# Norm factors of q and k: from GpSimd's power to ScalarE's logarithm and exponential with a Newton step on VectorE, and new due times for the planner

## The chip, the cores and the metric

The kernel runs on one core of one Trainium2 chip. Its time is the device time in microseconds (us) of one execution; of several executions the median is given. A profiled execution adds a trace: every instruction of TensorE (PE; PEld is its weight load), VectorE (DVE), ScalarE (ACT) and GpSimd (POOL), and the DMA issues of SyncE (SP), with start and duration.

## The reference

Attention with normalised q and k, for 8 batches of 12 heads, 448 positions and 64 columns a head, then a two-layer network with `h * cos(h)` between its matmuls:

```python
def rmsnorm(x, g):
    rms = np.sqrt(np.mean(x * x, axis=-1, keepdims=True) + 1e-06)
    return x / rms * g
q_n, k_n = (rmsnorm(q, g_q), rmsnorm(k, g_k))
scores = scale * np.matmul(q_n, k_n.transpose(0, 1, 3, 2))
scores = scores - np.max(scores, axis=-1, keepdims=True)
attn = np.exp(scores)
attn = attn / (np.sum(attn, axis=-1, keepdims=True) + 1e-09)
return np.matmul(attn, v)
...
h = x @ w_in          # 3584 x 768 by 768 x 2048
g = h * np.cos(h)
return g @ w_out
```

All tensors are 32-bit floats. What this case is about is `1 / rms`, one factor for each row of q and of k.

## The kernel before

**Units of work.** Two heads make a pair; there are 48 pairs, 6 for each batch. Pairs 0 to 5 are "plain" (32-bit matmuls without a split), pairs 6 to 47 split each operand into a high and a low part. For each pair the kernel prepares q and k (`prepare`), then attends (`attend`: scores, row minimum, exponential, transposes, product with v). `multiply` is the first matmul of the network for a batch; its result goes to memory. A second part, behind the attention pool, does `h * cos(h)` and the second matmul; the diff does not touch it.

**The factors.** For pairs 2 to 47, `st_square` (ACT) squares a tile `sd` of 128 x 14 x 64, `st_reduce` (DVE) sums it over 64 into `r` (128 x 14: seven columns for q, seven for k), and `st_pow` (POOL, L396 to L400) adds the small constant and raises to the power -0.5. Pairs 0 and 1 have 7 columns in `r`, and for k a path of their own: `kn_square`, `kn_reduce`, `kn_pow` (L426 to L429) on `rn` (112 x 8), then `kn_norm` (DVE, multiplies the rows of k), `kn_turn` (PE, transposes them) and `kn_copy` (ACT), and only then the scores. From pair 2 on, the k half of `r` goes to memory (`st_store`), comes back spread over the partitions (`rk_spread` into `D`, or `rk_load`), and `k_norm` (POOL) multiplies k by it into the tile `km` or in place. The q half of `r` is used in `rowmin` (DVE, L572), which multiplies the scores by it and takes the row minimum; `expo` (ACT, L580) follows.

**The order.** Each step is an entry with an engine, a cost, a due time, and the buffers that it reads and writes (`add`). `Plan.order` keeps a queue for each engine: of the entries that are ready when the engine is free, the one with the earliest due time goes next. What comes out is a fixed order of instructions for each engine; on the chip each engine takes them strictly in that order. Due times come from `base(u)` (13 apart for the plain pairs, 19 for the others) plus a table, `SHIFT`, with three numbers for each step (late pairs, the first split pairs, the plain pairs or the first network block), plus `PAIR` for single pairs; `BEGIN` moves the earliest start of loads. The weights of the network arrive as 64-bit numbers and are decoded in four steps on ACT, POOL, DVE and DVE (`decode`, L264, L267, L269, L271), among the early attention.

```python
def st_pow(u):
    n = st_cols(u)
    r = pair[u]["r"][:, :n]
    nc.gpsimd.tensor_scalar(r, r, 1.0, D * 1e-6, op0=ALU.mult, op1=ALU.add)
    nc.gpsimd.tensor_tensor(r, r, nhalf.broadcast_to([128, n]), ALU.pow)
```

Of the kernel before, what the change touches and what calls it, by code (L numbers as in the profile page):

```python
# [170 lines left out]
def tile_attention_moe(  # L171
# [11 lines left out]
    nc = tc.nc  # L183
# [212 lines left out]
    def st_pow(u):  # L396
        n = st_cols(u)
        r = pair[u]["r"][:, :n]
        nc.gpsimd.tensor_scalar(r, r, 1.0, D * 1e-6, op0=ALU.mult, op1=ALU.add)
        nc.gpsimd.tensor_tensor(r, r, nhalf.broadcast_to([128, n]), ALU.pow)  # L400
# [25 lines left out]
    def kn_pow(u):  # L426
        r = pair[u]["rn"][:KB]
        nc.gpsimd.tensor_scalar(r, r, 1.0, D * 1e-6, op0=ALU.mult, op1=ALU.add)
        nc.gpsimd.tensor_tensor(r, r, nhalf[:KB].broadcast_to([KB, 8]), ALU.pow)  # L429
# [406 lines left out]
    def y_store(b, oc, src):  # L836
# [10 lines left out]
        "k_norm": (47.04, -6.7, 6.09), "kn_copy": (0.0, 0.0, -26.03), "kn_load": (0.0, 0.0, -2.19),
        "kn_norm": (0.0, 0.0, 3.59), "kn_pow": (0.0, 0.0, -0.07), "kn_reduce": (0.0, 0.0, -6.89),
        "kn_square": (0.0, 0.0, 8.12), "kn_turn": (0.0, 0.0, -1.84), "kq_load": (-19.1, -5.97, 0.0),
        "m_place": (16.85, -8.49, 0.0), "pt_copy0": (0.0, 0.0, 23.54), "pt_copy1": (0.0, 0.0, 24.72),  # L850
        "pt_high0": (-18.32, 9.46, 0.0), "pt_high1": (-67.92, -9.7, 0.0), "pt_low0": (-20.7, 22.61, 0.0),
        "pt_low1": (-7.13, -11.08, 0.0), "q_high": (-127.36, -6.2, 0.0), "q_load": (0.0, 0.0, 72.1),
        "q_low": (-2.05, -0.3, 0.0), "q_scale": (-31.45, -11.91, 0.0), "rk_load": (8.49, 36.82, 0.0),
        "rk_spread": (0.0, 0.0, 11.66), "rowmin": (32.13, 70.56, 15.65), "rs_copy": (17.64, 0.91, 3.82),
        "rs_load": (-3.79, 6.46, 0.16), "rs_store": (8.77, 0.0, 5.61), "rsum": (-17.77, -6.78, 29.09),
        "score": (-0.07, -13.79, 0.0), "score_plain": (0.0, 0.0, -12.75), "st_load": (9.08, -3.06, -1.37),
# [5 lines left out]
        "w_decode": (208.02, 0.0, 0.0), "w_load": (3.35, 0.0, 0.0), "w_low": (13.11, 0.0, 0.0),
        "x_half": (4.91, 0.31, 0.0), "x_norm": (3.99, -11.02, 0.0), "x_plain": (0.0, 0.0, -20.3),
        "x_split": (-12.03, 9.82, 0.0), "x_sum": (7.41, -3.55, 0.0),
    }
    PAIR = (-10.16, 0.63, -1.81, -2.95, 0.29, 13.98, -17.36, -34.9, -15.47, 2.79, -35.19, -0.07)
    BEGIN = {"v_load": -14.52, "v_fetch": -9.53, "st_load": -5.75, "w_load": 12.81, "v_plain": 7.79, "kq_load": -31.08, "q_load": 2.47, "k_load": 4.72}

    def add(eng, cost, due, fn, *args, **more):
# [484 lines left out]
```

## Time and profile before

| what | value |
|---|---|
| median of 3 executions | 1363.93 us (1362.8 to 1364.56) |
| profiled execution, its own time | 1364.09 us |
| its span, first to last instruction | 1362.3 us |
| PE, DVE, ACT, POOL busy, share of the span | 98%, 75%, 68%, 47% |
| mean granted clock of TensorE | 0.997 of full speed |

Busy time counts an engine as busy while any of its instructions runs. The row of clock digits on the page shows 9 (full) throughout; a finer view of single stretches shows where it was lower. POOL has work only up to about 873 us; behind that only the second part of the network runs.

### The profile page before, as it was taken

The page shows a single profiled execution, that of the slowest core. Times are in us where ns is not written, and L with a number is a line of the kernel's source. Part 1 is how long each engine was busy: PE and PEld are TensorE (multiplying, and loading weights), DVE is VectorE, ACT ScalarE, POOL GpSimd, SP SyncE. Part 2 cuts the span into 40 slices and gives each one's busy share as a digit, 9 for nine tenths or more (in the row PEclk, how much of TensorE's full clock was granted, in tenths as well). Part 3 has the DMA queues.
Part 4 walks back from the last instruction along what each step waited for, and adds up shares of the span by engine and source line. Part 5 has one row for each costly group of instructions (what it writes and reads, how often), then busy time and mean ns, then how long its engine had stood idle before and what let it go on. Part 6 is the DMA issues. An engine that isn't in the chain of part 4 may idle for free.

```text
span 1362.3 us, 21541 instructions
## 1 busy us (share of the span) xinstructions
PE 1339.2 (98%) x6998; PEld 1172.5 (86%) x6998; DVE 1020.4 (75%) x1795; ACT 923.9 (68%) x1872; POOL 645.5 (47%) x570
## 2 busy tenths in 40 slices
PE   6998999999999999999999999999999999999998
PEld 3446888989899889898999998899999999999998
DVE  6888998777777777677677767517889789789743
ACT  6678778778877877877877786646666366366321
POOL 5789777767866877866876675320000000000000
PEclk9999999999999999999999999999999999999999
DMA  6798878889889798899888877258989369369334
GB/s 208 238 293 237 186 180 225 244 230 253 236 232 238 220 232 234 215 244 238 217 208 232 221 203 212 88 192 276 334 283 314 108 246 317 106 245 313 108 113 153
DMA packets 149472, 302.19 MB, mean 222 GB/s; under 512 B 34368, under 2 KB 83088, under 8 KB 149360
## 3 DMA queue, kind: packets, MB, share of 16 engines
q1 hardware_dynamic: 149360, 300.83, 76.2%
q8 instruction: 55, 0.90, 0.3%
q14 instruction: 57, 0.47, 0.1%
HBM read 193.99 MB, written 62.73 MB: 188 GB/s over the span
## 4 chain that ended last, share of the span: by engine, by line
PE 86%; POOL 4%; DVE 4%; ACT 2%; issue 2%; DMA 1%; SPq 0%; POOLq 0%; ACTq 0%; DVEq 0%
PE y L819 10%; PE y L821 10%; PE y L820 10%; PE ph L745 9%; PE ph L746 9%; PE ph L747 9%; PE S L568 8%; PE PT L614 7%; PE O L661 4%; PE O L663 3%; POOL r L400 1%; DVE S L572 1%; PE y L746 1%; PE y L747 1%; PE y L745 1%
## 5 line engine op out<-in xcount | busy, mean ns | idle before, releaser
L572 DVE TENSOR_SCALAR_CACHE_REDUCE S<-S,r 128x448 f32<-128x448 f32 x336 | 226.6, 688 | 96.3 <-PE S L568 85.3
L745 PE MATMUL ph<-xs,wi 128*128 128x448 f32 x660 | 250.3, 379 | 1.2 <-ACT hbuf L763 1.2
L580 ACT ACTIVATE P<-S,sm 128x448 f32<-128x448 f32 x336 | 213.1, 638 | 50.3 <-DVE S L572 45.0
L820 PE MATMUL y<-g,wo 128*128 128x448 f32 x672 | 245.4, 365 | 0.0
L819 PE MATMUL y<-g,wo 128*128 128x448 f32 x672 | 245.4, 365 | 0.0
L821 PE MATMUL y<-g,wo 128*128 128x448 f32 x672 | 245.4, 365 | 0.0
L746 PE MATMUL ph<-xs,wi 128*128 128x448 f32 x660 | 241.8, 366 | 0.0
L747 PE MATMUL ph<-xs,wi 128*128 128x448 f32 x660 | 241.6, 366 | 0.0
L801 ACT CAST g<-gq 128x896 fp32r<-128x896 f32 x112 | 105.7, 944 | 173.2 <-PE y L821 172.7
L637 ACT CAST hi<-PT 128x512 fp32r<-128x512 f32 (+1 forms) x336 | 169.3, 534 | 64.2 <-PE PT L621 41.5
L799 DVE TENSOR_TENSOR g<-gq,g 128x896 fp32r<-128x896 f32 x112 | 122.0, 1089 | 62.5 <-ACT g L801 62.1
L644 DVE TENSOR_TENSOR lo<-PT,hi 128x512 fp32r<-128x512 f32 x252 | 147.0, 617 | 26.1 <-ACT hi L637 25.3
L614 PEld LDWEIGHTS PT<-ident,P 128*128 128x128 f32 x1008 | 121.1, 140 | 40.1 <-issue 4.9
L614 PE MATMUL PT<-ident,P 128*128 128x128 f32 x1008 | 148.3, 274 | 4.3 <-ACT hi L671 1.6
L745 PEld LDWEIGHTS ph<-xs,wi 128*128 128x128 f32 x660 | 124.1, 188 | 17.1 <-ACT hbuf L763 2.5
L819 PEld LDWEIGHTS y<-g,wo 128*128 128x128 f32 x672 | 126.2, 188 | 10.0
L820 PEld LDWEIGHTS y<-g,wo 128*128 128x128 f32 x672 | 126.2, 188 | 10.0
L821 PEld LDWEIGHTS y<-g,wo 128*128 128x128 f32 x672 | 126.2, 188 | 9.9
L747 PEld LDWEIGHTS ph<-xs,wi 128*128 128x128 f32 x660 | 124.0, 188 | 11.0
L746 PEld LDWEIGHTS ph<-xs,wi 128*128 128x128 f32 x660 | 124.3, 188 | 9.1 <-POOL xs L729 0.2
L400 POOL TENSOR_TENSOR r<-r,nhalf 128x14 f32<-128x14 f32 (+1 forms) x48 | 125.8, 2620 | 4.0
L661 PE MATMUL O<-hi,vs 128*128 128x448 f32 x336 | 119.8, 372 | 0.0
(125 smaller groups left out, 2592.9 us busy)
## 6 DMA issues: line engine op xcount, KB each, us to landing
wo<-wo_d SPq DMA_DIRECT2D x152, 384.0 KB
gq<-h_d SPq DMA_DIRECT2D x64, 448.0 KB
h_d<-hbuf SPq DMA_DIRECT2D x54, 448.0 KB
wo_d<-ao SPq DMA_DIRECT2D x56, 384.0 KB
sd<-sd SPq DMA_DIRECT2D x46, 448.0 KB
kq<-kq SPq DMA_DIRECT2D x42, 480.0 KB
D<-qhi SPq DMA_DIRECT2D x84, 192.0 KB
raw<-w_in SPq DMA_DIRECT2D x16, 768.0 KB
```

The source lines that it names most:

```text
L572: nc.vector.tensor_scalar(d["S", t][:, :S], d["S", t][:, :S], d["r"][:, t : t + 1], None, op0=ALU.mult, op1=ALU.min, accum_out=d["sm"][:, ...
L580: nc.scalar.activation(p_rows(u, t), d.pop(("S", t))[:, :S], AF.Exp, bias=sm[:, 1, t : t + 1], scale=-1.0, accum_out=sm[:, 2, t : t + 1],)
L614: nc.tensor.transpose(pt[part][:, i * 128 : i * 128 + 128], p_rows(u, t)[:, c : c + 128], ident)
L637: nc.scalar.copy(hi if kc < 3 else hi[:64], pt_rows(u, kc, part))
L644: nc.vector.tensor_tensor(lo, src, hi.bitcast(F32), ALU.subtract)
L661: nc.tensor.matmul(O, st, d["hi", kc][:, HEADS[hh]], start=(kc == 0), stop=(kc == 3))
L745: nc.tensor.matmul(ph[:, :S], whi, x2[:, 0, :], start=(cc == 0), stop=False)
L746: nc.tensor.matmul(ph[:, :S], whi, x2[:, 1, :], start=False, stop=False)
L747: nc.tensor.matmul(ph[:, :S], wlo, x2[:, 0, :], start=False, stop=(cc == NCC - 1))
L819: nc.tensor.matmul(y, whi, hi[:, e], start=first and e == 0, stop=False, **more)
L820: nc.tensor.matmul(y, whi, lo[:, e], start=False, stop=False, **more)
L821: nc.tensor.matmul(y, wlo, hi[:, e], start=False, stop=last and e == NG - 1, **more)
```

## The change

`st_pow` and `kn_pow` on POOL go. In their place stand two steps each: a guess on ACT (logarithm with a scale of 2^-30 and a bias of the small constant, then exponential with -0.5, two activations of 7, 14 or 8 columns) and a Newton step on DVE (three instructions). The guess is written to a tile of its own (`r0` or `rm`), the Newton step writes the factor into `r` or `rn`. The factor comes out as -2 times what it was; `g_fold` takes that back with -0.25. One activation table that holds both functions is loaded at the start. The due times (`SHIFT`, `PAIR`, `BEGIN` and single coefficients) all have new numbers, and three costs of the planner change (POOL's decode step 1.3 to 2.0 and 0.7 to 1.05, `w_low` 0.6 to 0.53).

```diff
+    nc.scalar.preload_act_table_set("natural_log_exp_and_others")
     make_identity(nc, ident)
...
-    nhalf = cpool.tile([128, 1], F32, tag="nhalf", name="nhalf")
-    nc.vector.memset(nhalf, -0.5)
+    eps = cpool.tile([128, 1], F32, tag="eps", name="eps")
+    nc.vector.memset(eps, D * 1e-6 * 2.0**-30)
+    back = cpool.tile([128, 1], F32, tag="back", name="back")
+    nc.vector.memset(back, -15.0 * math.log(2.0))
...
-            gs[:, 4:6], gs[:, 0:2], -float(D) / math.sqrt(D), gs[:, 2:4], op0=ALU.mult, op1=ALU.mult
+            gs[:, 4:6], gs[:, 0:2], -0.25 * float(D) / math.sqrt(D), gs[:, 2:4], op0=ALU.mult, op1=ALU.mult
...
-    def st_pow(u):
+    def guess(x, g):
+        p = x.shape[0]
+        nc.scalar.activation(g, x, AF.Ln, bias=eps[:p], scale=2.0**-30)
+        nc.scalar.activation(g, g, AF.Exp, bias=back[:p], scale=-0.5)
+
+    def newton(x, g, t):
+        nc.vector.tensor_tensor(t, g, g, ALU.mult)
+        nc.vector.scalar_tensor_tensor(t, x, D * 1e-6, t, op0=ALU.add, op1=ALU.mult)
+        nc.vector.scalar_tensor_tensor(x, t, -3.0, g, op0=ALU.add, op1=ALU.mult)
+
+    def st_guess(u):
         n = st_cols(u)
...
+        guess(pair[u]["r"][:, :n], tl(u, "r0", [128, 28], F32)[:, :n])
+
+    def st_newton(u):
+        n = st_cols(u)
+        g = pair[u]["r0"]
+        newton(pair[u]["r"][:, :n], g[:, :n], g[:, 14 : 14 + n])
...
-        "st_pow": (-46.04, 0.0, -0.24), "st_reduce": (66.77, -13.66, 5.24), "st_square": (2.5, -9.37, -2.91),
+        "score_plain": (0.0, 0.0, -10.49), "st_guess": (-10.09, 11.46, 0.0), "st_load": (35.76, 20.44, -28.45),
+        "st_newton": (-14.6, 5.0, -25.09), "st_pow": (-31.44, 0.0, -0.24), "st_reduce": (-12.62, -1.6, -4.34),
...
-            add(POOL, 1.9, D0 - 50, kn_pow, u, r=kb, w=rn + [("rm", u)])
+            add(ACT, 0.45, D0 - 50, kn_guess, u, r=kb + rn + [("rh", u)], w=[("rm", u)])
+            add(DVE, 0.45, D0 - 50, kn_newton, u, r=[("rm", u)], w=rn + [("rh", u)])
...
-        add(POOL, 2.25 if turned else 2.9, D0 - 34, st_pow, u, w=r)
+        add(ACT, 0.45, D0 - 34, st_guess, u, r=r, w=[("r0", u)])
+        add(DVE, 0.45, D0 - 33, st_newton, u, r=[("r0", u)], w=r)
```

Over the whole program the order of 48 + 2 such steps changes, and with the due times nearly every engine's order moves somewhere. Three places follow. In the rows, names with a number behind them are single buffers; in the changed file the line of a function is some 15 to 18 higher than before.

The first is ACT at the start of the program, before (the square of pair 0's k, L418; the squares for `r`, L391; the copies of `kn_copy`, L444; the first exponential, L580):

```order
L418 ACTIVATE PT_109<-kq 112x256 x2
L391 ACTIVATE sd_116<-sd_116 128x448
L418 ACTIVATE PT_110<-kn_118 112x512
L391 ACTIVATE sd_116<-sd_116 128x448
L444 ACTIVATE kn_102<-PT_109,gs 128x224 x2
L444 ACTIVATE kn_102<-PT_109,gs 64x64
L580 ACTIVATE P,sm_154<-S_0_155,sm_154 128x448
```

and with the change (L401 and L402 are the two activations of a guess):

```order
L434 ACTIVATE PT_112<-kq 112x256 x2
L394 ACTIVATE sd_119<-sd_119 128x448
L401 ACTIVATE rm_133<-rn_129,eps 112x8
L402 ACTIVATE rm_133<-rm_133,back 112x8
L434 ACTIVATE PT_113<-kn_121 112x512
L401 ACTIVATE r_142<-r_136,eps 128x7
L402 ACTIVATE r_142<-r_142,back 128x7
L394 ACTIVATE sd_119<-sd_119 128x448
L462 ACTIVATE kn_105<-PT_112,gs 128x224 x2
L462 ACTIVATE kn_105<-PT_112,gs 64x64
L401 ACTIVATE rm_160<-rn_153,eps 112x8
L402 ACTIVATE rm_160<-rm_160,back 112x8
```

The first guess stands behind the square of `sd`, and the guess for pair 1's k behind the three copies that the first scores need.

The second is DVE in the same stretch, before (sums, L394 and L424; `kn_norm`, L434; `rowmin`, L572):

```order
L424 TENSOR_REDUCE rn_126<-PT_109 112x4 x2
L394 TENSOR_REDUCE r_132<-sd_116 128x7
L434 TENSOR_TENSOR kq<-kq,rn_126 112x256 x2
L424 TENSOR_REDUCE rn_140<-PT_110 112x8
L394 TENSOR_REDUCE r_152<-sd_116 128x7
L572 TENSOR_SCALAR S_0_155,sm_154<-S_0_155,r_132 128x448
L434 TENSOR_TENSOR kn_118<-kn_118,rn_140 112x512
```

and with the change, from the second instruction of pair 0's Newton step for `r` (L405 to L407 are a Newton step; ahead of these rows stand the same two sums, a Newton step for `rn`, and `kn_norm`):

```order
L406 SCALAR_TENSOR_TENSOR r_142<-r_136,r_142 128x7
L407 SCALAR_TENSOR_TENSOR r_136<-r_142 128x7
L440 TENSOR_REDUCE rn_153<-PT_113 112x8
L397 TENSOR_REDUCE r_163<-sd_119 128x7
L405 TENSOR_TENSOR rm_160<-rm_160 112x8
L406 SCALAR_TENSOR_TENSOR rm_160<-rn_153,rm_160 112x8
L407 SCALAR_TENSOR_TENSOR rn_153<-rm_160 112x8
L452 TENSOR_TENSOR kn_121<-kn_121,rn_153 112x512
L405 TENSOR_TENSOR r_173<-r_173 128x7
L406 SCALAR_TENSOR_TENSOR r_173<-r_163,r_173 128x7
L407 SCALAR_TENSOR_TENSOR r_163<-r_173 128x7
L590 TENSOR_SCALAR S_0_166,sm_165<-S_0_166,r_136 128x448
```

The first `rowmin` (L590 now) stands behind three more Newton steps than its own needs and behind `kn_norm` of pair 1, which it was ahead of.

The third is POOL from pair 2's factor to pair 2's k, before (L493 is `q_scale`, L267 the decode step of a weight block, L477 `k_norm` into `km`):

```order
L399 TENSOR_SCALAR r_186<-r_186 128x14
L400 TENSOR_TENSOR r_186<-r_186,nhalf 128x14
L493 TENSOR_SCALAR q_99<-q_99,gs 128x512
L267 COPY raw_200<-raw_200 128x768
L399 TENSOR_SCALAR r_277<-r_277 128x14
L400 TENSOR_TENSOR r_277<-r_277,nhalf 128x14
L267 COPY raw_225<-raw_225 128x768
L477 TENSOR_TENSOR km_104<-kq,D_100 128x448
L477 TENSOR_TENSOR km_104<-kq,D_100 64x64
```

and with the change:

```order
L511 TENSOR_SCALAR q_102<-q_102,gs 128x512
L270 COPY raw_218<-raw_218 128x768
L495 TENSOR_TENSOR km_107<-kq,D_103 128x448
L495 TENSOR_TENSOR km_107<-kq,D_103 64x64
L511 TENSOR_SCALAR q_102<-q_102,gs 128x512
L270 COPY raw_236<-raw_236 128x768
L495 TENSOR_TENSOR km_108<-kq,D_104 128x448
L495 TENSOR_TENSOR km_108<-kq,D_104 64x64
```

Between `q_scale` and `km` there were two decode copies and a power; now there is one decode copy.

## Rows read from the trace of the kernel before

**Rows 1.** The page, busy us, share of the span and instructions of each engine.

```profile
PE 1339.2 (98%) x6998; PEld 1172.5 (86%) x6998; DVE 1020.4 (75%) x1795; ACT 923.9 (68%) x1872; POOL 645.5 (47%) x570
```

**Rows 2.** Busy time by stretch: PE, PEld, DVE, ACT, POOL, then clock, DMA, GB/s.

```profile
20.00:110.00 90.00, 85.56 (x379) 40.26 (x377) 74.24 (x163) 67.40 (x158) 72.49 (x53) 0.98 0.87 265
110.00:190.00 80.00, 75.14 (x406) 64.61 (x405) 76.36 (x146) 64.43 (x144) 64.65 (x51) 1.00 0.81 192
190.00:820.00 630.00, 629.69 (x3495) 565.86 (x3494) 465.24 (x1002) 490.47 (x1153) 460.29 (x417) 1.00 0.87 229
820.00:1362.30 542.30, 538.77 (x2700) 496.95 (x2698) 394.68 (x460) 290.36 (x395) 36.48 (x35) 1.00 0.63 213
```

**Rows 3.** Timeline of the first 13 us: start, us, instruction, idle time before it.

```profile
5.42 1.66 POOL L429 TENSOR_TENSOR rn<-rn,nhalf 112x8 f32<-112x8 f32 x1
5.84 0.58 ACT L391 ACTIVATE sd<-sd 128x448 f32<-128x448 f32 x1 [1.58 <-DMA sd<-sd]
6.44 0.62 DVE L394 TENSOR_REDUCE r<-sd 128x7 f32<-128x448 f32 x1 [1.40 <-ACT sd L391]
...
7.11 0.76 DVE L434 TENSOR_TENSOR kq<-kq,rn 112x256 f32<-112x256 f32 x2
...
7.64 0.98 PE L439 MATMUL PT<-ident,kq 112*128 112x112 f32 x4 [7.64 <-DVE kq L434]
...
7.98 0.69 DVE L424 TENSOR_REDUCE rn<-PT 112x8 f32<-112x512 f32 x1
...
8.71 1.12 ACT L444 ACTIVATE kn<-PT,gs 128x224 f32<-128x224 f32 x3 [0.85 <-ACT sd L391]
...
9.55 3.69 PE L552 MATMUL S<-kn,q 64*128 64x448 f32 x8 [0.93 <-ACT kn L444]
...
11.55 0.69 DVE L572 TENSOR_SCALAR_CACHE_REDUCE S<-S,r 128x448 f32<-128x448 f32 x1 [2.35 <-POOL r L399]
...
12.16 0.69 DVE L434 TENSOR_TENSOR kn<-kn,rn 112x512 f32<-112x512 f32 x1
```

**Rows 4.** Groups of instructions by form: busy us, mean ns of one, idle before.

```profile
L400 POOL TENSOR_TENSOR r<-r,nhalf 128x14 f32<-128x14 f32 x46 | 122.8, 2669 | 3.8
...
L588 ACT ACTIVATE sm<-sm 128x7 f32<-128x7 f32 x48 | 10.1, 210 | 1.0
L590 DVE RECIPROCAL sm<-sm 128x7 f32<-128x7 f32 x48 | 9.6, 200 | 25.8 <-ACT sm L588 25.6
...
L418 ACT ACT_TABLE_LOAD x1 | 1.3, 1283 | 0.7 <-PEq L1344 0.7
```

**Rows 5.** Timeline of POOL from 29 us, then of PE behind it.

```profile
29.49 3.28 POOL L400 TENSOR_TENSOR r<-r,nhalf 128x14 f32<-128x14 f32 x1
32.71 1.91 POOL L267 COPY raw<-raw 128x768 uint16<-128x768 uint16 x1
34.45 1.72 POOL L477 TENSOR_TENSOR km<-kq,D 128x448 f32<-128x448 f32 x2
...
30.96 1.72 PE L679 MATMUL O<-hi,vs 128*64 128x448 f32 x4
32.61 0.98 PE L614 MATMUL PT<-ident,P 128*128 128x128 f32 x7
35.63 1.61 PE L552 MATMUL S<-km,q 64*128 64x448 f32 x4 [2.04 <-POOL km L477]
```

**Rows 6.** Busy time by stretch as in rows 2, around that wait.

```profile
30.00:40.00 10.00, 7.96 (x32) 3.30 (x31) 8.58 (x17) 6.74 (x15) 9.65 (x8) 0.87 0.46 143
40.00:50.00 10.00, 10.00 (x47) 4.92 (x48) 8.05 (x22) 6.62 (x19) 6.24 (x5) 0.96 0.84 294
```

**Rows 7.** Instructions of two lines, min/median/max ns: L271 from 20 to 200, L400 from 110 to 190.

```profile
L271 DVE SCALAR_TENSOR_TENSOR aq<-aq,raw x8: 941/959/1905, 36.4 to 183.8; 128x768 int32<-128x768 int32 x8
...
L400 POOL TENSOR_TENSOR r<-r,nhalf x4: 2750/2786/2899, 122.9 to 176.9; 128x14 f32<-128x14 f32 x4
```

**Rows 8.** Groups by form as in rows 4: the decode copies of the large form.

```profile
L267 POOL COPY raw<-raw 128x768 uint16<-128x768 uint16 x16 | 32.6, 2037 | 14.4 <-ACT wf L264 11.9 <-ACT aq L264 2.5
```

More of the change, by code (lines that the diff above doesn't have):

```diff
@@ L424, in kn_reduce, with kn_guess, kn_newton @@
         nc.vector.tensor_reduce(pair[u]["rn"][:KB, 2 * a : 2 * b], sq, axis=AX.X, op=ALU.add)
[L426 to L429, printed above, removed]
+    def kn_guess(u):
+        guess(pair[u]["rn"][:KB], tl(u, "rm", [128, 16], F32)[:KB, :8])
+    def kn_newton(u):
+        g = pair[u]["rm"][:KB]
+        newton(pair[u]["rn"][:KB], g[:, :8], g[:, 8:])
     def kn_norm(u, a, b):
@@ L847, in tile_attention_moe @@
[L847 to L856, printed above, removed]
@@ L862, in tile_attention_moe @@
[L862 to L867 removed]
+        "av": (6.06, 97.39, 0.0), "av3": (-16.63, -7.14, 0.0), "av_plain": (0.0, 0.0, 15.8),
@@ L882, in add @@
         if name in ("w_load", "w_decode", "w_high", "w_low"):
-            due += -0.295 * first
+            due += -0.413 * first
         if name in ("ffn1", "h_out", "h_store", "h_both") and not first:
-            due += -0.468 * args[1]
+            due += -0.229 * args[1]
         if name in ("v_fetch", "v_decode", "v_sum", "v_split", "v_store"):
-            due += -8.68 + 25.297 * first
+            due += -4.26 + 25.441 * first
         other = ("w_load", "w_decode", "w_high", "w_low", "v_fetch", "v_decode", "v_sum", "v_split", "v_store", "e_clear")
@@ L891, in add @@
         if more.get("start"):
-            late = BEGIN.get(name0, 0.0) + (-0.147 * first if name0 == "w_load" else 0.0)
+            late = BEGIN.get(name0, 0.0) + (-0.337 * first if name0 == "w_load" else 0.0)
             more["start"] = max(0.0, more["start"] + late)
+        if name0 in ("w_decode", "w_rebias") and first > 1:
+            more["start"] = max(more.get("start", 0.0), 0.0 + 0.0 * first)
         cost *= {DVE: 1.059, ACT: 1.026, POOL: 1.021}.get(eng, 1.0)
@@ L917, in weights @@
         if f64:
-            for step, eng, cost in ((0, ACT, 0.84), (1, POOL, 1.3), (2, DVE, 0.74), (3, DVE, 1.0)):
+            for step, eng, cost in ((0, ACT, 0.84), (1, POOL, 2.0), (2, DVE, 0.74), (3, DVE, 1.0)):
                 add(eng, cost, d - 8.0 + step, w_decode, fc, step,
@@ L922, in weights @@
         for hf in range(2):
-            add(DVE, 0.6, d, w_low, fc, hf, nc.vector, r=[f, w], w=[("wlo", fc, hf)])
+            add(DVE, 0.53, d, w_low, fc, hf, nc.vector, r=[f, w], w=[("wlo", fc, hf)])
     SPLITS = (
@@ L938, in weights2 @@
                 add(SP, ISS, e - 20.0, v_fetch, c, k, w=[st], kb=384.0, start=e - 30.0)
-                for step, eng, cost in ((0, ACT, 0.45), (1, POOL, 0.7), (2, DVE, 0.5), (3, DVE, 0.65)):
+                for step, eng, cost in ((0, ACT, 0.45), (1, POOL, 1.05), (2, DVE, 0.5), (3, DVE, 0.65)):
                     add(eng, cost, e + step, v_decode, c, k, step,
@@ L978, in prepare @@
             for h, k in zip(halves, hs):
-                add(DVE, 0.06 + 0.63 * sh, D0 - 50, kn_reduce, u, *h, r=[k, *kb], w=[("rn" if h[0] == 0 else "rm", u)])
-            add(POOL, 1.9, D0 - 50, kn_pow, u, r=kb, w=rn + [("rm", u)])
+                add(DVE, 0.06 + 0.63 * sh, D0 - 50, kn_reduce, u, *h, r=[k, *kb], w=[("rn" if h[0] == 0 else "rh", u)])
+            add(ACT, 0.45, D0 - 50, kn_guess, u, r=kb + rn + [("rh", u)], w=[("rm", u)])
+            add(DVE, 0.45, D0 - 50, kn_newton, u, r=[("rm", u)], w=rn + [("rh", u)])
             for h, k in zip(halves, hs):
```

36 lines of the change are left out of this document (24 added, 12 removed), and 2 rows, old and new, of the table RING.

## The prediction, made before the changed kernel had run

> **What bounds the kernel now.** I read the page first, then busy time by stretch, then the timeline where TensorE (PE) is idle. The page says that PE is busy 1339.2 us of a span of 1362.3 [rows 1]: about 23 us are all that can be won by waiting less. The stretches say where they lie [rows 2]. From 190 to 820 us PE is busy 629.69 of 630, and behind 820, 538.77 of 542.3, with no power left in it. So nothing that this change does can help there. From 20 to 110 us PE is idle 90 - 85.56 = 4.4 us, from 110 to 190 us 80 - 75.14 = 4.9 us; the rest, some 10 us, lies in the first 20, above all ahead of PE's first instructions at 7.64 and 9.55 us [rows 3].
>
> The same stretches show who keeps PE waiting. POOL is busy 72.49 of 90 us, then 64.65 of 80; DVE 74.24 of 90, then 76.36 of 80, the fullest of the engines beside PE between 110 and 190 us [rows 2]. A power of 14 columns takes POOL 2.67 us [rows 4], more than a decode copy of 768 columns with 2.04 us [rows 8]. So the change takes work from an engine that is full early, and gives some to one that is nearly full a little later. Behind 190 us both have room: POOL 460.29 of 630, DVE 465.24.
>
> **The change part by part.** The sum is made against the profiled execution, 1364.1 us, which is 0.2 above the median of the runs shown.
>
> *Work removed and added.* POOL loses 46 powers of 2.67 us (122.8 us, [rows 4]), and some small ones. ACT gets two small activations for each factor. The nearest row is an activation of 7 columns with 0.21 us [rows 4]; the far end above is the square of 448 columns with 0.58 us [rows 3]. I take 0.21, which has the same few columns: 0.42 us for a guess. DVE gets three small instructions for each; the nearest row is a reciprocal of 7 columns with 0.20 us [rows 4], so 0.6 us for a Newton step. A far end above is worked out below. From 190 to 820 us some 33 pairs add 33 x 0.42 = 14 us to ACT and 33 x 0.6 = 20 us to DVE, which are idle there for 140 and 165 us while PE never waits: cost nothing. If that cover were gone, the most it could cost is those 20 us.
>
> The Trainium skill, page "ScalarE: Activation LUTs", section "What ACT_TABLE_LOAD costs", gives an activation with a bias from memory about 280 ns and 0.83 ns for each column, some 0.29 us here, against 186 ns with a constant bias. By that the opening below would be some 0.2 us later, and nothing else would change; the row, whose bias is a constant, does not show it.
>
> *The opening, until about 13 us.* Before: POOL's power for pair 0's k ends at 5.42 + 1.66 = 7.08, DVE multiplies at 7.11, PE starts at 7.64 and the first scores at 9.55 us [rows 3]. The guess could start when the power did, at 5.42 us at the latest, but ACT's order puts it behind the square of `sd`, which waits for its DMA until 5.84 and ends at 6.42 [rows 3]. So the guess runs from 6.42 to 6.84. DVE meanwhile takes the sum of `sd`, which ends at 7.06 [rows 3]; the Newton step runs from 7.06 to 7.66. The multiplication starts at 7.66 instead of 7.11, 0.55 us **later**, and with it PE (8.2) and the first scores (10.1). On DVE then come that multiplication (0.76, to 8.42), a Newton step (0.6, to 9.02), and the sums of `rn` (0.69, [rows 3]) and of pair 1's `sd` (0.62, like pair 0's [rows 3]), to 10.33. The next Newton step needs a guess that stands on ACT behind the three copies, which before ended at 8.71 + 1.12 = 9.83 [rows 3] and now at 10.38; with 0.42 for the guess that is 10.80. DVE waits from 10.33 to 10.80, then Newton 0.6, multiplication 0.69 [rows 3], Newton 0.6: the first row minimum starts at 12.69 instead of 11.55, 1.14 us later. Against that, the multiplication of pair 1 is already done, which before ran from 12.16 on behind the first row minimum; the second row minimum slips from 12.16 + 0.60 = 12.76 only to 12.69 + 0.61 = 13.30, by 0.54 us. Between 0.54 and 1.14 I take **+0.8 us**. The ends for the range are 0, if waits further on take it in, and +1.2.
>
> *Pair 2's k.* PE waits 2.04 us for `km` until 35.63 [rows 5]. On POOL a power of 3.28 us and a decode copy of 1.91 stand directly ahead of `km` [rows 5]. In the new order both are gone from there (the third place above): without them POOL could have begun `km` some 5 us earlier, before PE came to the end of its work at 33.6 [rows 5]. PE now comes to these scores without the product of 1.72 us and the transposes of 0.98 us that ran ahead of them [rows 5], 2.7 us sooner; 5 is more than 2.7, and the 0.8 of the opening falls on both sides. So the wait goes: **-2.0 us**. Behind that wait the granted clock falls: 0.87 in the mean from 30 to 40 us and 0.96 from 40 to 50 [rows 6], so PE, otherwise at 2.4 GHz, ran at 1.2 for a while after having been idle. What that cost is 10 x 0.13 + 10 x 0.04 = 1.7 us of full clock, all of it on the path, as PE was busy throughout the second of these stretches. Without the idle time I take the clock to stay up: **-1.7 us**. Both can stay at 0.
>
> *The other waits of PE from 20 to 190 us.* Together 4.4 + 4.9 - 2.0 = 7.3 us. They end at copies on ACT and subtractions on DVE, whose queues are in turn behind decode steps that come from POOL. The ends are 0 (all stay) and -7.3 (all go). I take two fifths, as POOL is only one of three engines that are full here (POOL 0.81, DVE 0.82, ACT 0.75 of the first stretch): **-2.9 us**.
>
> *More work on DVE from 110 to 190 us.* There are four factors in this stretch [rows 7], and DVE is idle for 3.6 us [rows 2]. At 0.6 us each, 2.4 us, it is hidden. But a DVE instruction with two inputs from on-chip memory can take much longer while POOL works: L271 has a median of 0.96 and a maximum of 1.905 us [rows 7], 0.95 more. With one of three instructions so held up a Newton step is 1.55 us, four are 6.2, and 2.6 more than the idle time. Between 0 and +2.6 I take **+0.9 us**, nearer to 0, since medians are far more frequent than maxima.
>
> The Trainium skill, "GPSIMD Engine Reference", section "1. Specifications", speaks against this change here: it says that GpSimd's way to on-chip memory is shared with VectorE, and that they contend where a VectorE instruction has two inputs there. All three Newton instructions have two. By this rule the term would be at its upper end; the maximum in the row agrees that something holds such instructions up, its median says not often.
>
> **The sum:** 0.8 - 2.0 - 1.7 - 2.9 + 0.9 = -4.9, so 1364.1 - 4.9 = **1359.2 us**. The forecast's own range is 1356.5 to 1361.5.
>
> **The rivals.** About 0.2%, 2.7 us, is what a measurement of this kernel can tell from no change; its bounds are 1361.2 and 1366.7.
>
> *All of PE's waits from 20 to 190 us came from POOL.* For it: POOL is busy 9.65 of 10 us from 30 to 40 [rows 6]. Against it: DVE is as full, and gets more. Time: 1364.1 + 0.8 - 3.7 - 7.3 = 1353.9 us.
>
> *A new wait takes the place of the old.* Pair 2's `km` comes early, but the scores then wait for the exponentials to empty their banks, since ACT and DVE are later by the opening and have guesses and Newton steps in their queues; the other waits stay, and the clock falls all the same. For it: DVE and ACT take their steps strictly in order, and DVE already stood still for a guess in the opening as worked out. Against it: it needs ACT or DVE to lose as much as POOL wins. Half of the 2.0 stays, all of the 1.7 and the 7.3: 1364.1 + 0.8 - 1.0 = 1363.9 us, no change.
>
> *DVE becomes the bound from 110 to 190 us, slower.* Two of three Newton instructions held up: 0.6 + 2 x 0.95 = 2.5 us a factor, four are 10, less 3.6 us idle: 6.4 us on the path. With the other waits not won back, 1364.1 + 0.8 - 3.7 + 6.4 = 1367.6 us. For it: DVE's 76.36 of 80 us, and that every Newton step stands between row minima for which ACT and PE wait. Against it: medians. It turns into a loss when a step with its waits costs over (3.6 + 2.9) / 4 = 1.6 us, and one of over 0.2% at (3.6 + 2.9 + 2.7) / 4 = 2.3 us.
>
> *The change doesn't do what it says:* ACT would load a table for every change of function, 1.283 us each [rows 4], about 96 of them, 120 us. The order of the changed program has two loads, as before, so this gets no chance.
>
> **How the numbers follow.** Forecast 0.46, all waits gone 0.10, a new wait 0.25, DVE as the bound 0.19. The first two are faster by over 0.2%, but for some of the forecast's upper edge, which the third's lower edge makes up for: faster 0.56, same 0.25, slower 0.19. For the range I leave out the lower end of the second case and the upper half of the last: 1354 to 1367.5 us.
>
> **What would show it.** Right: the first scores at about 10.1 and the first row minimum at about 12.7 us; no wait of PE for `km` near 33 us, and a clock of 1.00 from 30 to 50 us; PE idle for about 4 to 6 us from 20 to 190 us instead of 9.3; POOL's busy time down by some 140 us; Newton instructions near 0.2 us in the median. Wrong: Newton instructions of 0.5 us or more in the mean; DVE over 78 of 80 us from 110 to 190 with more idle time of PE; a further stretch of low clock; or PE idle anywhere between 190 and 820 us.

## The result, and the profile after

The changed kernel takes **1378.22 us** (median of 4 runs, 1377.7 to 1378.49), the kernel before 1364.21 in the same runs: a ratio of 1.0104 [1.0087, 1.0122], slower by 14 us where 5 us less was forecast. The profiled execution has a span of 1375.9 us, 13.6 more than before. The page's first line, then busy time by stretch (columns as in rows 2), of the changed kernel:

```profile
PE 1350.8 (98%) x6998; PEld 1171.5 (85%) x6998; DVE 1067.5 (78%) x1946; ACT 946.4 (69%) x1972; POOL 506.0 (37%) x470
```

```profile
20.00:110.00 90.00, 86.29 (x382) 39.71 (x380) 80.41 (x182) 70.39 (x172) 48.97 (x40) 1.00 0.89 286
110.00:190.00 80.00, 73.77 (x393) 61.67 (x393) 78.16 (x149) 64.98 (x146) 51.15 (x42) 1.00 0.71 179
190.00:820.00 630.00, 628.47 (x3484) 564.10 (x3483) 506.49 (x1125) 508.35 (x1229) 374.12 (x355) 1.00 0.82 231
820.00:1375.90 555.90, 552.38 (x2726) 501.07 (x2724) 391.53 (x454) 290.23 (x395) 30.37 (x29) 1.00 0.61 204
```

Against [rows 1, 2], POOL has lost 139.5 us and DVE has gained 47.1. From 110 to 190 us DVE is busy 78.16 of 80 and PE idle 6.2 us, where it was 4.9. From 190 to 820 us PE is idle 1.5 us, where it was 0.3. And PE itself is **busy 11.6 us longer with the same 6,998 matmuls**.

The opening is as it was forecast. The timeline of the changed kernel, to be held against [rows 3]:

```profile
8.21 0.98 PE L457 MATMUL PT<-ident,kq 112*128 112x112 f32 x4 [8.21 <-DVE kq L452]
...
10.06 3.69 PE L570 MATMUL S<-kn,q 64*128 64x448 f32 x8 [0.88 <-ACT kn L462]
...
12.73 0.69 DVE L590 TENSOR_SCALAR_CACHE_REDUCE S<-S,r 128x448 f32<-128x448 f32 x1
```

So is pair 2's `km`: its scores start without a wait, and the clock from 30 to 50 us is full [rows 5, 6]. The timeline of PE and two stretches, changed kernel:

```profile
34.02 1.02 PE L570 MATMUL S<-km,q 64*128 64x448 f32 x4
```

```profile
30.00:40.00 10.00, 10.00 (x45) 4.12 (x44) 9.19 (x23) 9.43 (x25) 5.22 (x5) 1.00 0.76 219
40.00:50.00 10.00, 9.79 (x48) 4.63 (x47) 8.67 (x20) 6.77 (x18) 3.62 (x4) 1.00 0.72 231
```

The new instructions, groups by form (busy us, mean ns, idle before), and min/median/max of the first of the Newton step's three:

```profile
L406 DVE SCALAR_TENSOR_TENSOR r<-r,r 128x14 f32<-128x14 f32 x46 | 18.0, 392 | 1.6
L405 DVE TENSOR_TENSOR r<-r 128x14 f32<-128x14 f32 x46 | 16.3, 355 | 2.6 <-ACT r L402 1.9
L401 ACT ACTIVATE r<-r,eps 128x14 f32<-128x14 f32 x46 | 14.4, 312 | 4.8 <-DVE r L397 4.6
L402 ACT ACTIVATE r<-r,back 128x14 f32<-128x14 f32 x46 | 14.1, 308 | 1.5
L407 DVE SCALAR_TENSOR_TENSOR r<-r 128x14 f32<-128x14 f32 x46 | 11.0, 238 | 1.6
```

```profile
L405 DVE TENSOR_TENSOR r<-r x48: 151/174/1557, 8.2 to 817.4; 128x14 f32<-128x14 f32 x46, 128x7 f32<-128x7 f32 x2
```

A guess takes 0.62 us, a Newton step 0.355 + 0.392 + 0.238 = 0.985 us in the mean. The mean of one Newton instruction is up to 2.3 times its median of 0.17 us.

Where the 13.6 us arise shows when the same matmul is compared. Weight loads of the first network part and matmuls of the second, by line: number, min/median/max ns, first and last start. Before:

```profile
L745 PEld LDWEIGHTS ph<-xs,wi x660: 186/188/192, 105.3 to 901.8; 128*128 128x128 f32 x165
...
L819 PE MATMUL y<-g,wo x672: 362/365/369, 950.0 to 1358.0; 128*128 128x448 f32 x168
```

Changed:

```profile
L763 PEld LDWEIGHTS ph<-xs,wi x660: 186/188/192, 106.0 to 906.4; 128*128 128x128 f32 x165
...
L837 PE MATMUL y<-g,wo x672: 368/368/368, 955.6 to 1371.6; 128*128 128x448 f32 x168
```

At 105 us the changed kernel is 0.7 us behind, at the first `y` matmul 5.6, at the last 13.6. The last 8 us come in a part where PE waits for nothing and no new instruction runs: 2,016 equal matmuls take 408.0 us before and 416.0 after. Every one lasts 368 ns now, where they lasted 362 to 369. Their starts, kernel before and changed kernel:

```profile
1000.09 0.36 PE L820 MATMUL y<-g,wo 128*128 128x448 f32 x1
1000.30 0.36 PE L821 MATMUL y<-g,wo 128*128 128x448 f32 x1
1000.50 0.37 PE L819 MATMUL y<-g,wo 128*128 128x448 f32 x1
1000.70 0.36 PE L820 MATMUL y<-g,wo 128*128 128x448 f32 x1
1000.90 0.36 PE L821 MATMUL y<-g,wo 128*128 128x448 f32 x1
```

```profile
1000.22 0.37 PE L837 MATMUL y<-g,wo 128*128 128x448 f32 x1
1000.43 0.37 PE L838 MATMUL y<-g,wo 128*128 128x448 f32 x1
1000.63 0.37 PE L839 MATMUL y<-g,wo 128*128 128x448 f32 x1
```

In nanoseconds, from the start of one to the next: 203, 202, 203, 199, 207 and again from the front before, a mean of 202.7; 206.7 for each after. I call them the quick and the even **rhythm**. In the changed kernel the even one sets in at 890.7 us, behind the last two `O` matmuls of its line 679, and only matmuls of this one shape come until the end. In the kernel before, the same place leads into the quick one.

### The profile page after: what moved, and what is told of

It is laid out like the page before. It is cut to its first block, busy times and chain, and to the rows that moved or that the text cites. A ratio compares the mean times of both kernels' runs of the same rounds, so it can differ in the third digit from the quotient of the medians.

```text
span 1375.9 us, 21578 instructions
## 1 busy us (share of the span) xinstructions
PE 1350.8 (98%) x6998; PEld 1171.5 (85%) x6998; DVE 1067.5 (78%) x1946; ACT 946.4 (69%) x1972; POOL 506.0 (37%) x470
## 4 chain that ended last, share of the span: by engine, by line
PE 86%; DVE 8%; ACT 2%; issue 2%; DMA 1%; POOL 1%; SPq 0%; DVEq 0%; POOLq 0%; ACTq 0%
PE y L838 10%; PE y L839 10%; PE y L837 10%; PE ph L763 8%; PE ph L764 8%; PE ph L765 8%; PE S L586 8%; PE PT L632 7%; PE O L679 4%; PE O L681 3%; DVE S L590 2%; PE y L765 1%; PE y L763 1%; PE y L764 1%; PE S L570 1%
## 5 line engine op out<-in xcount | busy, mean ns | idle before, releaser
L590 DVE TENSOR_SCALAR_CACHE_REDUCE S<-S,r 128x448 f32<-128x448 f32 x336 | 225.6, 685 | 55.0 <-PE S L586 49.7
L655 ACT CAST hi<-PT 128x512 fp32r<-128x512 f32 (+2 forms) x336 | 174.9, 531 | 42.2 <-PE PT L632 19.2
L662 DVE TENSOR_TENSOR lo<-PT,hi 128x512 fp32r<-128x512 f32 (+1 forms) x252 | 153.4, 618 | 41.4 <-ACT hi L655 39.6
L679 PE MATMUL O<-hi,vs 128*128 128x448 f32 x336 | 125.1, 380 | 2.8 <-DVE hi L664 2.5
L586 PE MATMUL S<-M,D 128*128 128x448 f32 x252 | 101.8, 404 | 1.3 <-ACT P L598 1.3
```

Of the source, the lines that this page charges most:

```text
L586: nc.tensor.matmul(d["S", t][:, :S], a, c, start=(i == 0), stop=(i == len(ops) - 1))
L590: nc.vector.tensor_scalar(d["S", t][:, :S], d["S", t][:, :S], d["r"][:, t : t + 1], None, op0=ALU.mult, op1=ALU.min, accum_out=d["sm"][:, ...
L655: nc.scalar.copy(hi if kc < 3 else hi[:64], pt_rows(u, kc, part))
L679: nc.tensor.matmul(O, st, d["hi", kc][:, HEADS[hh]], start=(kc == 0), stop=(kc == 3))
```

## The experiments

Two questions: what sets the rhythm (8 to 9 us), and what costs the 4 to 5 us ahead of it. All runs were timed beside the kernel before, whose median was 1363.9 to 1364.8 us.

### Is it where the tiles lie?

The two new constants take a slot of 32 bytes more, which moves all later tiles. Two runs move them: the changed kernel with both constants in one tile, and the kernel before with an unused tile.

```diff
-    eps = cpool.tile([128, 1], F32, tag="eps", name="eps")
+    both = cpool.tile([128, 2], F32, tag="both", name="both")
+    eps, back = both[:, 0:1], both[:, 1:2]
...
-    back = cpool.tile([128, 1], F32, tag="back", name="back")
```

> The changed kernel, with its two constants (eps and back) as two columns of one tile, so that all later tiles lie 32 bytes lower, where they lay in the kernel before; order and work are unchanged. Theory A (the pitch of the fp32 matmuls of the second network part depends on where their operands lie): the steady matmul pitch of that part falls from 206.7 to about 202.7 ns, 2,016 matmuls give back some 8 us and the time is 1368 to 1371 us, still slower than before by the 5 us lost ahead of 950 us. Theory B (the pitch goes with the new order of the work or with the run): pitch stays 206.7 and the time 1377 to 1379. Busy VectorE, the opening and the clock stay as in the changed kernel by both.

```diff
+    pad = cpool.tile([128, 1], F32, tag="pad", name="pad")
+    nc.vector.memset(pad, 0.0)
```

> The kernel before, with one unused 128x1 tile among the constants, so that all later tiles lie 32 bytes higher, as in the changed kernel. Theory A (placement sets the pitch): the second network part slows to a pitch of 206.7 ns and the time rises by about 8 to 9 us, to 1371 to 1374 us. Theory B (order of the work): 1363 to 1366, pitch 202.7.

The first took 1368.51 us, ratio 1.0033 [1.0021, 1.0045], at 202.7 ns. The second took 1371.93, at 206.7 in its profile. Both are theory A's numbers. Yet eight executions of the second took 1370.8 to 1375.1 us and two 1363.0 and 1363.4: one program, one placement, both times. So placement alone does not decide. Two more runs say the same: each swaps operations or due times alone, with the weights and rows of these matmuls where they lay before.

```diff
 (new operations, old due times: the tables SHIFT, PAIR, BEGIN and the costs of the kernel before, and)
+        "st_guess": (-46.04, 0.0, -0.24), "st_newton": (-46.04, 0.0, -0.24),
+        "kn_guess": (0.0, 0.0, -0.07), "kn_newton": (0.0, 0.0, -0.07),
```

> The new operations (logarithm, exponential, Newton step) with the due times, start times and costs of the kernel before, and with the two constants in one tile, so tiles lie as before. Theory 1 (what is lost ahead of 950 us comes from the VectorE time of the Newton step): VectorE stays over 77.5 us busy of the 80 from 110 to 190, and the time is 1367 to 1371. Theory 2 (the new due times lose it): VectorE falls back to about 76.5 to 77 there and the time is 1362 to 1366. Theory B of the pitch says nothing new here: 202.7 ns by both.

> The old power on GpSimd with the due times, start times and costs of the changed kernel; tiles lie as before. Theory 1 (VectorE time of the Newton step loses the time ahead of 950 us): VectorE about 76.4 us busy of 80 from 110 to 190, time 1362 to 1366. Theory 2 (the new due times lose it): 1367 to 1371. If the steady pitch of the second network part is 206.7 ns here and in the kernel with one tile, the new order and not the placement makes it (Theory B), and the time is 8 us higher.

They took 1402.88 us, 1.0282 [1.0262, 1.0302], and 1374.99, 1.0079 [1.0054, 1.0103]. The matmuls of the first, then of the second:

```profile
L837 PE MATMUL y<-g,wo x672: 368/368/368, 982.2 to 1398.3; 128*128 128x448 f32 x168
```

```profile
L819 PE MATMUL y<-g,wo x672: 362/365/369, 962.3 to 1370.3; 128*128 128x448 f32 x168
```

The even rhythm in the first, with the operands where the quick one ran: theory A falls, and so does theory B, as the new due times alone run quick. Theories 1 and 2 both missed: each swap costs more than both together (32 and 12 us by the start of `y`, against 5.6). The due times belong to their operations; neither run tells what one of the two is worth. What exactly the old due times hold up with the new operations was not followed further.

### A short matmul

Theory R: a stream of equal matmuls keeps the rhythm that uneven ones ahead of it left. The edit puts one matmul of 32 columns, which is then overwritten, ahead of the blocks from about 900 us on.

```diff
     def ffn1_block(b, fc, bank):
+        if fc == NEAR:
+            nc.tensor.matmul(banks[bank][:, :32], wts[("wi", fc)][:, 0, :128], xs["t"][:, 0, 0, :32], start=True, stop=True)
```

> The changed kernel with one more matmul of 32 columns ahead of the first block of the part that runs from about 896 us to the end; its sum is overwritten, tiles and order are unchanged. Theory R (the matmul stream keeps one of two rhythms, a steady pitch of 206.7 ns or a cycle of five that averages 202.7, for as long as nothing but the same matmul comes, and which one is left over from the last uneven matmuls before it): a short matmul, behind which nearly every stream of the traces so far has taken the faster rhythm, gives 202.7 from there on, and 2,300 matmuls by 4 ns, 9 us, come back: 1368 to 1370 us. Theory A (placement of the operands): pitch stays 206.7 and the time 1378 to 1379.

> The kernel before with the unused constant tile (which gave 1371 to 1375 us in eight executions and 1363 in two) and the same short matmul. Theory R: all executions at 1363 to 1366 us, pitch 202.7. Theory A: mostly 1371 to 1375 as without the short matmul.

**1368.88 us** (9 executions, 1367.4 to 1370.5), 1.0034 [1.0024, 1.0044], and 1362.83 (10 executions, 1361.7 to 1366.7), 0.9994 [0.9985, 1.0004]. PE of the changed kernel with the short matmul:

```profile
910.07 0.37 PE L764 MATMUL S<-xs,wi 128*128 128x448 f32 x1
910.27 0.37 PE L765 MATMUL S<-xs,wi 128*128 128x448 f32 x1
910.48 0.18 PE L769 MATMUL y<-xs,wi 128*128 128x32 f32 x1
910.51 0.45 PE L763 MATMUL y<-xs,wi 128*128 128x448 f32 x1
910.79 0.36 PE L764 MATMUL y<-xs,wi 128*128 128x448 f32 x1
910.99 0.36 PE L765 MATMUL y<-xs,wi 128*128 128x448 f32 x1
911.18 0.37 PE L763 MATMUL y<-xs,wi 128*128 128x448 f32 x1
```

Even ahead of it, quick behind it, with order and placement unchanged. The numbers are theory R's: the rhythm cost the changed kernel 1378.22 - 1368.88 = 9.3 us, as much as over 2,300 matmuls by 4.0 ns. That uneven matmuls are what sets the rhythm is not shown by it. From here on the short matmul stays in, and the remaining 4.6 us are the object.

### The Newton step

> The changed kernel with the short matmul and without the three VectorE instructions of each Newton step (the guess is taken as it is, the constant factor adjusted; this leaves out the correction of the logarithm's and exponential's error). The order of all other work is as in the changed kernel. Theory D (the 4 us lost ahead of 950 us beside the rhythm come from the VectorE time of the Newton step, 46 pairs by about 1 us, of which 7 before 110 us and 4 from 110 to 190): VectorE falls by 4 us of 80 from 110 to 190 and the time is 1364 to 1366, 3 to 5 below the kernel with the short matmul alone. Theory O (the new order loses it): not over 1 us below that kernel.

**1358.79 us**, 0.9963 [0.995, 0.9976]: 10.1 us less than with the step, twice of what theory D said, and less than the kernel before. Its stretches:

```profile
20.00:110.00 90.00, 87.37 (x388) 40.71 (x388) 76.94 (x167) 73.06 (x179) 49.88 (x42) 1.00 0.93 293
110.00:190.00 80.00, 77.61 (x429) 67.49 (x428) 77.73 (x146) 68.16 (x154) 53.00 (x41) 1.00 0.75 185
190.00:820.00 630.00, 629.77 (x3502) 567.14 (x3501) 481.01 (x1024) 511.26 (x1236) 380.03 (x360) 1.00 0.82 232
```

From 110 to 190 us DVE is still at 77.73 of 80, but it gets through other work in that time: PE is idle 2.4 us, not 6.2. What PE waits for there (us, times, longest) shows it. The waits for DVE's subtractions (`lo`, `hi`), with the step and the short matmul:

```profile
PE PT L632 <- DVE lo L662: 2.8, 3, 2.1
PE PT L637 <- DVE lo L662: 0.7, 1, 0.7
PE O L679 <- DVE hi L664: 0.6, 1, 0.6
```

and without the step:

```profile
PE PT L635 <- DVE lo L660: 0.4, 1, 0.4
PE PT L630 <- DVE lo L660: 0.2, 1, 0.2
```

Together 4.1 us against 0.6; in the kernel before they were 3.4. Doses and another engine for the step:

```diff
 (two VectorE instructions)
-        nc.vector.tensor_tensor(t, g, g, ALU.mult)
+        nc.scalar.activation(t, g, AF.Square)
 (five)
+        for _ in range(2):
             nc.vector.tensor_tensor(t, g, g, ALU.mult)
             nc.vector.scalar_tensor_tensor(t, x, D * 1e-6, t, op0=ALU.add, op1=ALU.mult)
 (on GpSimd)
+        nc.gpsimd.tensor_tensor(t, g, g, ALU.mult)
+        nc.gpsimd.tensor_tensor(t, x, t, ALU.mult)
+        nc.gpsimd.tensor_scalar(t, t, 1.0, -3.0, op0=ALU.mult, op1=ALU.add)
+        nc.gpsimd.tensor_tensor(x, t, g, ALU.mult)
```

> The changed kernel with the short matmul, and the square of the guess moved from VectorE to ScalarE: two VectorE instructions in a Newton step, not three, and one more of ScalarE. With three instructions the kernel with the short matmul took 1368.9 us, with none 1358.8. Theory D (the VectorE time of these instructions costs, each about a third of the 10.1 us): 1364 to 1367 us. Rival L (what costs is the wait of VectorE's queue on the guess, which gets 0.3 us longer here): 1369 to 1372.

> The same with three VectorE instructions, the first two done twice to the same result: five in all. Theory D: 1374 to 1378 us (6.7 above 1368.9, if it is in proportion). Rival L (the wait for the guess costs, not the instructions): 1369 to 1371.

> The changed kernel with the short matmul and the whole Newton step on GpSimd, as four instructions (the small constant is left out of the step's own sum and stands in the guess alone). Theory D: VectorE is freed as without the step, 1358 to 1362 us, unless GpSimd is late. Rival L (the chain from the sums to the first row minimum is what counts, or GpSimd's queue, longer by over 1 us a pair): 1366 us or more.

| VectorE instructions in a step | us | ratio to before |
|---|---|---|
| 0, step left out | 1358.79 | 0.9963 [0.995, 0.9976] |
| 0, step on GpSimd | 1362.56 | 0.9989 [0.9979, 0.9998] |
| 2 | 1364.21 | 0.9998 [0.9989, 1.0008] |
| 3 | 1368.88 | 1.0034 [1.0024, 1.0044] |
| 5 | 1388.0 | 1.0176 [1.0157, 1.0194] |

Rival L falls: two instructions, behind a longer guess, are faster, and five, behind the same guess, slower by 19 us. Theory D has the right cause and the wrong law: an instruction costs 2.7 us between 0 and 2, 4.7 from 2 to 3 and 9.6 beyond. That DVE's idle time takes in the first ones, and less is left for each further one, would fit, but no run shows it. On GpSimd the step costs 3.8 us instead of 10.1, although it has four instructions there.

Does the cost lie where DVE is full? Two runs leave the step out on one side of about 198 us:

```diff
+    def bare(u):
+        return u < 14
...
-        nc.scalar.activation(g, g, AF.Exp, bias=back[:p], scale=-0.5)
+        nc.scalar.activation(x if bare(u) else g, g, AF.Exp, bias=(back2 if bare(u) else back)[:p], scale=-0.5)
```

> The changed kernel with the short matmul, and the Newton step left out for the first 14 pairs, those whose step runs before about 198 us (16 of the 50 steps; the guess is used as it is there, with the factor in its exponential). With all steps 1368.9 us, with none 1358.8. Theory P (place: the cost lies where VectorE is full, ahead of 198 us; the two traces part by 6.4 us up to 193 us): 1362 to 1363.5. Rival N (a cost for each step, wherever it is, 10.1 us by 16 of 50): 1365 to 1366.5.

> The same with the Newton step kept for the first 14 pairs and left out for the others (34 of the 50 steps, behind about 198 us). Theory P: 3.3 us come back, 1364.5 to 1366.5; were the prediction right that these cost nothing: 1368 to 1370. Rival N (10.1 us by 34 of 50): 1361 to 1363.

1371.91 us, 1.0055 [1.0039, 1.0072], and 1374.52, 1.0073 [1.0058, 1.0088]: both above the kernel with all steps, which no theory had. The first of them around the short matmul:

```profile
904.03 0.37 PE L771 MATMUL S<-xs,wi 128*128 128x448 f32 x1
904.24 0.36 PE L772 MATMUL S<-xs,wi 128*128 128x448 f32 x1
904.44 0.18 PE L776 MATMUL y<-xs,wi 128*128 128x32 f32 x1
904.47 0.45 PE L770 MATMUL y<-xs,wi 128*128 128x448 f32 x1
904.76 0.37 PE L771 MATMUL y<-xs,wi 128*128 128x448 f32 x1
904.97 0.37 PE L772 MATMUL y<-xs,wi 128*128 128x448 f32 x1
```

Here the short matmul found the quick rhythm and left the even one; the second matmul behind it starts 0.29 us after the first, 0.28 above. The new constant `back2` had moved the tiles by 32 bytes. With `back2` as a second column of `back`'s tile they lie as in the changed kernel:

> The run with the Newton step left out for the first 14 pairs, with the new constant as a second column of an older tile, so that all tiles lie 32 bytes lower, at multiples of 64 bytes as in the changed kernel. Theory K (behind the short matmul the stream takes the faster rhythm where the tiles lie at multiples of 64 bytes): pitch 202.7, 8 us less than the 1371.9 of the last run, and with theory P (place of the steps) 1362 to 1364.5. Without theory K: 1371 to 1373.

> The same for the run that leaves the step out for all but the first 14 pairs. Theory K: pitch 202.7 and 1365.5 to 1367.5 us; the prediction's claim that the steps behind 190 us cost nothing would hold only if it stood at 1368 or above. Without theory K: 1373.5 to 1375.5.

> The kernel before with nothing but the short matmul added; its tiles lie 32 bytes beside multiples of 64. Theory K: the stream, which runs at 202.7 ns in the kernel before, is put into the slower rhythm, 206.7 ns, and the time is 1371 to 1374 us. If the short matmul gives the faster rhythm wherever the tiles lie: 1363 to 1366.

1362.41 us, 0.9987 [0.9977, 0.9996]; 1366.0, 1.0012 [1.0002, 1.0022]; and 1363.89, 1.0002 [0.999, 1.0013]. All three run at 202.7 ns. So theory P holds: the first 16 steps cost 1368.88 - 1362.41 = **6.5 us**, the 34 behind 198 us **2.9**; together 9.4 of the 10.1. Theory K does not hold as stated: the kernel before with the short matmul has its tiles beside multiples of 64 bytes too, and stays quick. The short matmul left the quick rhythm in ten kernels and the even one in two, those whose weights and rows begin 32 bytes behind a multiple of 128. But these two also share what the matmul found: in eight of the twelve profiled executions the stream ahead of it was even, and all eight turned quick; in four it was quick, two of them stayed so, and these two turned even. Which of the two decides, the place or what went ahead, no run tells.

### One pair alone

The kernel before, order kept, with the new operations for one pair, whose power stood ahead of the `km` of [rows 5]; without and with the short matmul:

```diff
+    NEW = (3,)
...
+        if u in NEW:
...
+            nc.scalar.activation(g, r, AF.Ln, bias=eps, scale=2.0**-30)
+            nc.scalar.activation(g, g, AF.Exp, bias=back, scale=-0.5)
+            nc.vector.tensor_tensor(t, g, g, ALU.mult)
+            nc.vector.scalar_tensor_tensor(t, t, -0.5, r, op0=ALU.mult, op1=ALU.mult)
+            nc.vector.scalar_tensor_tensor(r, t, 1.5, g, op0=ALU.add, op1=ALU.mult)
+            return
```

> The kernel before, its order kept, with the logarithm, exponential and Newton step in place of the power for the fourth pair alone, whose power stood on GpSimd from 28.8 to 32.8 us ahead of the km on which TensorE waited 2.04 us. Theory W (that wait and the clock that fell behind it cost 2.0 and 1.7 us, and nothing takes their place): 1360 to 1362.5 us, no wait for km at 33.6, TensorE at the full clock from 37 to 41. Rival (another wait of the opening takes the place): 1363 to 1365.

> The kernel before with the new operations for the fourth pair alone, and the short matmul. Without the short matmul it ran at a pitch of 206.7 ns from 885 us on and took 1370.8. Theory R with a small gain of the opening: 1361 to 1364 us, pitch 202.7, about 1 us under the kernel before.

1370.79 us, 1.0048 [1.0032, 1.0064], in the even rhythm, which no theory had named for it; and 1362.4, 0.9983 [0.9973, 0.9994], in the quick one. The wait for `km` is gone in both. Two kernels keep the wait (1.8 us in each) and have the short matmul: the kernel before, 1363.89, and the one with the unused tile, 1362.83. Against these one pair alone gains 1.5 and 0.4 us by the medians, and 1.9 and 1.1 thousandths (2.6 and 1.5 us) by the ratios to the kernel before that was timed beside each. The intervals overlap, so this run does not tell how much of the 2.0 and 1.7 us comes back.

It does not tell where the clock's part belongs either. The wait in the kernel with the unused tile and the short matmul, and its stretch from 30 to 40 us:

```profile
PE S L554 <- POOL km L479: 1.8, 1, 1.8
```

```profile
30.00:40.00 10.00, 8.24 (x41) 3.83 (x39) 8.47 (x15) 6.98 (x15) 9.74 (x7) 1.00 0.47 153
```

The wait stands there nearly as in [rows 5], and the clock from 30 to 40 us is 1.00, not 0.87 [rows 6].

## Why the prediction was wrong

The forecast was -4.9 us, and +14.0 was measured. By the runs this is +9.3 for the rhythm, where the forecast had nothing, +10.1 for the Newton steps, where it had 0.9, and -5.5 for all else (1358.79 without the step, against 1364.3 for the kernel before beside it), where its other four terms gave -5.8. The last agreement is one of sums, and in part luck: no run separates the four, or the new due times from them, and the opening's +0.8 holds Newton steps too.

**"From 190 to 820 us PE is busy ... So nothing that this change does can help there"**, and behind 820 likewise: the step that failed most. I read a PE without idle time as a PE whose time is fixed. Two things were missed. The busy time of equal matmuls has two values, and over 2,300 of them from 890 us on keep the one they fall into: 9.3 us, shown by the short matmul. And the steps behind 198 us, put at "cost nothing" since DVE was idle there for 165 us, cost 2.9. Their upper end was given as 20 us and then left out of the range.

**"More work on DVE from 110 to 190 us", +0.9 us, 2.6 at most:** mis-sized, in the duration and in the price. The mean of all steps, 0.985 us, lies within the bounds of 0.6 and 1.55, but the four steps of this stretch took 6.9 us together in the changed kernel's trace, not 2.4 and not 6.2. Of its 150 Newton instructions 103 ran with no GpSimd instruction beside them, and none of these took over 0.18 us; all 29 of over 0.2 us, up to 1.6, overlap one. Here it is a decode copy:

```profile
141.92 1.92 POOL L270 COPY raw<-raw 128x768 uint16<-128x768 uint16 x1 [4.38 <-ACT wf L267]
142.06 1.55 DVE L406 SCALAR_TENSOR_TENSOR r<-r,r 128x14 f32<-128x14 f32 x1
```

As for the price, the first 16 steps cost 6.5 us. I set four steps against DVE's idle time of 3.6 us in one stretch, and gave the twelve ahead of 110 us no cost. But idle time is no store that a step can draw on. Of these 3.6 us, 2.9 were a single wait for a decode step of GpSimd, in the kernel before:

```profile
DVE raw L269 <- POOL raw L267: 2.9, 1, 2.9
```

Work that comes in elsewhere makes the next subtraction late, and PE waits for that: 4.1 us with the steps, 0.6 without. The rival "DVE becomes the bound", 1367.6 us at a chance of 0.19, comes nearest to what happened apart from the rhythm, 1368.9 us measured. That the two numbers agree so well is in part luck: the rival looked at these four steps alone, where 2.9 us came behind 198 us and a part ahead of 110.

The rule of the Trainium skill, "GPSIMD Engine Reference", section "1. Specifications", which was set against the median of [rows 7], proved the better guide: this case's trace agrees with it, with 29 long instructions of 29 beside one of GpSimd. The Trainium skill's page "ScalarE: Activation LUTs", section "What ACT_TABLE_LOAD costs", gives some 0.29 us (an estimate from its figures) for an activation with a bias from memory; 0.31 was measured, where I took 0.21 from a row with a constant bias.

**The clock, -1.7 us:** the cause was not shown by [rows 6], and the low level only moved. From 30 to 50 us the changed kernel has 1.00, as forecast. But so has the kernel with the unused tile and the short matmul from 30 to 40 us, although PE waits 1.8 us for `km` there. In these two executions the traces hold no record of the clock ahead of 22.8 and 21.4 us; the views show 1.00 for such a stretch, but the matmuls took the times of 1.2 GHz until then, scores of 64x448 about 950 to 1113 ns each. In the kernel before, the record begins at 13.5 us with the full level, and scores took 536 to 640 ns until it fell at 17 us. PE's scores, kernel before and changed kernel:

```profile
13.86 1.48 PE L552 MATMUL S<-kn,q 64*128 64x448 f32 x4
```

```profile
14.62 1.86 PE L570 MATMUL S<-kn,q 64*128 64x448 f32 x2
```

When the level rises and falls in the first 40 us differs between executions of the same work, so a change cannot be credited with one profile's dip. Nor do the totals show such a price: of 92 executions of the kernel before that ran beside the experiments, the 30 with a mean granted clock of 0.999 or more took 1363.8 us in the mean, the other 62 took 1364.4.

**Pair 2's `km`, -2.0 us, and two fifths of the other waits, -2.9:** the first wait went as forecast, but at 105 us the changed kernel stood at +0.7, where the terms up to there gave about -4 (the opening, `km`, the clock, and two fifths of the 2.4 us of other waits ahead of 110). It is no matter of one execution: the first weights of the network come at 103.5 to 105.3 us in four traces with the old order, at 105.1 to 106.5 in three with the changed one. In part this is the rival "a new wait takes the place of the old". PE was idle 9.9 us from 20 to 190 us, not 4 to 6 as forecast; without the Newton step it was 5.0.

**Right:** the first scores at 10.06 us (10.1 forecast) and the first row minimum at 12.73 (12.69); POOL's busy time down by 139.5 us (140); Newton instructions of 0.17 us in the median; no reloading of tables. That the first row minimum came out so close is in part luck: the guess ahead of it took 0.63 us, not 0.42, and VectorE's instructions behind it overlapped by about as much. Three of the signs named for a wrong forecast came true: DVE over 78 of 80 us with more idle time of PE, a further stretch of low clock, ahead of 22.8 us, and PE idle between 190 and 820 us.

Faster than both kernels is the changed kernel with the short matmul and without the Newton step, 1358.79 us, which gives up the step's correction. With the correction kept, the step on GpSimd (1362.56, without the small constant in the step) and one pair alone (1362.4), both with the short matmul, are about 0.1 to 0.2% under the kernel before, at the edge of what their intervals tell.

## What to carry to other kernels

Before explaining a difference of some 0.5% by the change, compare the duration of the same matmuls in both traces: if equal instructions without a wait have another median, the difference can be a rhythm that an edit elsewhere may flip, and one short matmul can show it (it turned eight even streams of eight quick, but two quick ones of four even). An engine's idle time is no room for new work unless the trace says what it is idle for, and small instructions with two inputs on VectorE are sized by what GpSimd does beside them, not by their median: cost instructions on the fullest engine beside TensorE by leaving them out and doubling them, not by their duration against its idle time. Due times tuned for one set of operations are no measure of another.

## What the runs showed of the hardware

Matmuls of 128x448 with a new weight for each ran in two rhythms at the full clock, 206.7 ns each or a cycle of 207, 203, 202, 203 and 199. Without interruption they stayed in it for over 2,300 matmuls. One program, the kernel before with an unused tile, showed totals of both kinds in ten executions (1371 to 1375 us eight times, 1363 twice). What puts a stream into one or the other was not settled.

VectorE instructions of 128x14 and less with two inputs took 0.15 to 0.18 us wherever no GpSimd instruction ran beside them (103 of 150 in the changed kernel), and up to 1.6 us beside one; 18 of 47 beside one stayed under 0.2.
